# One decode step of an adaptive-layer-norm block: grouped output-weight loads and a rearranged last stage

## The chip, the cores and the metric

The kernel runs on one core of a Trainium2 chip, all data in float32. The metric is the device time of one execution in microseconds (us). Before the change the median of 3 runs is 394.72 us (393.41 to 396.38).

## The reference

One token for each of 4 batch rows goes through attention against a cache and a small token mixer, both modulated by a condition vector `c`:

```python
mod = (silu(c) @ w_mod).reshape(4, 6, 1, 512)      # sa, ca, ga, sb, cb, gb
h = layernorm(x) * (1 + ca) + sa
x = x + ga * A(h)        # q = h @ wq; 32 query heads, 8 KV heads, 4096 cached keys, Dh 128;
                         # softmax(q k^T / sqrt(128)) v, then @ wo (4096 x 512)
h = layernorm(x) * (1 + cb) + sb
x = x + gb * B(h)        # u = gelu(layernorm(h) * w1 + b1), F = 1792 values for each channel;
                         # y = sum over F of u * w2, + b2
```

The key and value caches are 4 x 8 x 4096 x 128 each, 67 MB apiece; with `wq`, `wo` and `w_mod` some 157 MB are read once.

## The kernel before

Batch row and KV head make a pair `i = 8 b + h`, 32 pairs in all. A pair needs one key tile and one value tile of 2 MB, each 128 partitions x 16 KB. They pass through a ring of five slots (`ring`), which also holds `wq` and the pieces `wm` of `w_mod`; a load into a slot is issued when the slot's last reader is done. All loads are issued by SyncE (SP) in the order in which they are written: the first two parts of `w_mod`, the small vectors (`sm`), `x`, four pieces of `wq`, three key tiles, and from there key tile, value tile, and for the first eight pairs the 1 MB of `wo` of head `i` (`load_v`). `wo` stays in memory for all four batch rows.

The schedule is written out by hand (`manual_schedule`): each engine runs its instructions in program order. In front of the main loop DVE clears a number of buffers (L67 to L89), while `sm` is loaded; then ACT and DVE form silu(c) (L115 to L120), PE multiplies with `w_mod` (L133), and the queries follow (L148).

The loop over pairs staggers scores (L213), softmax (L224 to L236), transposes of the probabilities (L243), values (L265) and the output projection (`project_a`, `project_b`). Behind each batch row of eight pairs the generator `epilogue` does layer norm and mixer of that row in small steps, one at each `next(epi)`. Its last two steps are the contraction of the remaining tiles of `u` with `w2` on PE, and `ZK` (L441) on DVE.

The last pairs stand behind the loop, each step by hand. `finish` then does row 3, with nothing left to overlap except the last steps of row 2's `epilogue`: `stats` and `gather` (a matmul that spreads the statistics to all partitions) twice, around `adaln`; `bcast` (L364), which spreads the row over the partitions; `affine`, in which ACT centres it (`hb`, L375) and DVE folds the reciprocal deviation into `w1` (`wr`); then 14 tiles of 512 values: scale and shift (DVE, or for the first two ACT), gelu (ACT, L461 and L466) and contraction with `w2` (PE, L387). Last come gate, residual and stores.

In `affine` the centring is `hb = pb + nm` with `nm = -mean` as an instruction of its own:

```python
        def center():
            dv.tensor_scalar(nm, mean, -1.0, None, op0=OP.mult)
            nc.scalar.activation(hb, pb, AF.Identity, bias=nm)
```

Of the kernel before, what the change touches and what calls it, by code (L numbers as in the profile page):

```python
# [8 lines left out]
F32 = mybir.dt.float32  # L9
I32 = mybir.dt.int32  # L10
AF = mybir.ActivationFunctionType
OP = mybir.AluOpType
# [3 lines left out]
B, D, HQ, HKV, SK, DH, F = 4, 512, 32, 8, 4096, 128, 1792  # L16
REP = HQ // HKV
NF = F // 128
EPS = 1e-5
P = 128  # L20
# [8 lines left out]


@with_exitstack
def adaln_decode(ctx: ExitStack, tc: tile.TileContext, small, x, wmod, wq, kT, v, wo, out):
    nc = tc.nc
    pad = ctx.enter_context(tc.tile_pool(name="pad", bufs=1))
    ring = ctx.enter_context(tc.tile_pool(name="ring", bufs=5))
    wos = ctx.enter_context(tc.tile_pool(name="wos", bufs=1))
    cst = ctx.enter_context(tc.tile_pool(name="cst", bufs=1))
    wk = ctx.enter_context(tc.tile_pool(name="wk", bufs=2))
# [4 lines left out]
    ps_e = ctx.enter_context(tc.tile_pool(name="ps_e", bufs=1, space=PSUM))  # L43
    ctx.enter_context(tc.manual_schedule())
    mm = nc.tensor.matmul
    dv = nc.vector

    neg1 = pad.tile([1, 96], F32, name="neg1")[:, 0:1]
    sm = cst.tile([P, NSM], F32, name="sm")
    xr = cst.tile([B, D], F32, name="xr")  # L50
    wm01 = ring.tile([P, 2, 4, D], F32, name="wm01", tag="kv")
    nc.sync.dma_start(wm01, wmod[0:2].rearrange("t p k n -> p t k n"))
    nc.sync.dma_start(sm, small)
    nc.sync.dma_start(xr, x)
    wqt = []
    for k in range(4):
        t = ring.tile([P, HQ * DH], F32, name=f"wq{k}", tag="kv")
        nc.sync.dma_start(t, wq[k * P:(k + 1) * P, :])
        wqt.append(t)
    w1, b1, w2 = sm[:, 0:NF], sm[:, NF:2 * NF], sm[:, 2 * NF:3 * NF]  # L60
# [2 lines left out]

    ident = cst.tile([P, P], F32, name="ident")
    make_identity(nc, ident)
    ones = cst.tile([P, P], F32, name="ones")
    dv.memset(ones, 1.0)  # L67
    dv.memset(neg1, -1.0)
# [15 lines left out]
    for i in range(3):  # L84
        t = cst.tile([P, 16, 32], F32, name=f"pT{i}")
# [1 line left out]
        pTs.append(t)  # L87
    pTl = cst.tile([P, 8, 4, 32], F32, name="pTl")
    dv.memset(pTl, 0.0)  # L89
    wo_t = [wos.tile([P, REP, D], F32, name=f"wo{h}") for h in range(HKV)]  # L90
    prep = cst.tile([P, 4, P], F32, name="prep")
    osb = cst.tile([P, B, P], F32, name="osb")
    sT8 = cst.tile([P, 4, B, 8], F32, name="sT8")

    def rsqrt(ve, n, tag, beside=None, out=None, times=None):
        y = wk.tile([n, 1], F32, name="y" + tag)
        t = wk.tile([n, 1], F32, name="t" + tag)
        q = wk.tile([n, 1], F32, name="q" + tag)
        dv.tensor_scalar(y.bitcast(I32), ve.bitcast(I32), -0.5, RS0, op0=OP.mult, op1=OP.add)
        if beside:  # L100
            beside()
        dv.scalar_tensor_tensor(t, y, ve, y, op0=OP.mult, op1=OP.mult)
        dv.scalar_tensor_tensor(y, t, RS1, y, op0=OP.subtract, op1=OP.mult)
        dv.scalar_tensor_tensor(t, y, ve, y, op0=OP.mult, op1=OP.mult)
        if times is not None:
            dv.tensor_scalar(out, times, y, None, op0=OP.mult)
        dv.scalar_tensor_tensor(q, t, RS2, t, op0=OP.subtract, op1=OP.mult)
        if times is not None:
            dv.scalar_tensor_tensor(out, q.to_broadcast(list(out.shape)), RS3, out, op0=OP.add, op1=OP.mult)
            return out  # L110
        dv.scalar_tensor_tensor(y, q, RS3, y, op0=OP.add, op1=OP.mult)
        return y
# [56 lines left out]
    def load_wm(t):  # L169
        n = 1 if t >= 4 else 2  # L170
        w = ring.tile([P, n, 4, D], F32, name=f"wm{t}", tag="kv")
        nc.sync.dma_start(w, wmod[t:t + n].rearrange("t p k n -> p t k n"))
        for e in range(n):
            WM[t + e] = w[:, e]

# [5 lines left out]
    def load_v(i):  # L181
        b, h = divmod(i, HKV)
        VT[i] = ring.tile([P, 32, DH], F32, name=f"v{i}", tag="kv")
        src = v[b, h].rearrange("(p j) d -> p j d", p=P)
        cuts = (0, 16, 24, 28, 32) if i == NS - 1 else (0, 16, 32) if i >= NS - 3 else (0, 32)
        for lo, hi in zip(cuts, cuts[1:]):
            nc.sync.dma_start(VT[i][:, lo:hi], src[:, lo:hi])
        if i < HKV:
            nc.sync.dma_start(wo_t[i], wo[i])
        if i == 2 or i == 4:  # L190
            load_wm(i)
        if i == NS - 1:
            load_wm(5)

    def modmm(pm, t):
        for k in range(4):
            for c in range(4):
                mm(pm[32 * c:32 * c + 32, :], sT8[:, k].rearrange("p b r -> p (b r)"),
                   WM[t][:, k, c * P:(c + 1) * P], start=(k == 0), stop=(k == 3))
# [132 lines left out]
    def stats(xin, b):  # L332
        st = wk.tile([P, 6], F32, name="st")
        dv.bn_stats(st, xin)
        sm_ = wk.tile([P, 4, 6], F32, name="stm")
        dv.tensor_mul(sm_, st.unsqueeze(1).to_broadcast([P, 4, 6]), ident.rearrange("p (c r) -> p c r", c=4)[:, :, 8 * b:8 * b + 1].to_broadcast([P, 4, 6]))
        return sm_

    def gather(sm_):
        pst = ps_m.tile([P, 24], F32, name="pst", tag="m")  # L340
        mm(pst, ones[0:1, :], epsr.rearrange("p a b -> p (a b)"), start=True, stop=False)
        mm(pst, ones, sm_.rearrange("p a b -> p (a b)"), start=False, stop=True)
        return pst

    def norm(pst):
        mv = wk.tile([P, 2], F32, name="mv")
        dv.bn_aggr(mv, pst)
        return mv[:, 0:1], mv[:, 1:2]

    def adaln(b, pst):  # L350
        mean, var = norm(pst)
        a = wk.tile([P, P], F32, name="a")
        h1 = wk.tile([P, P], F32, name="h1")
        r = rsqrt(var, P, "e", lambda: dv.scalar_tensor_tensor(
            a, XK[:, b], mean, prep[:, 3], op0=OP.subtract, op1=OP.mult))
        dv.scalar_tensor_tensor(h1, a, r, prep[:, 2], op0=OP.mult, op1=OP.add)
        return h1, stats(h1, b)

    def bcast(h1, b, pb=None):
        if pb is None:  # L360
            pb = ps_e.tile([P, 4, P], F32, name="phb", tag="e")
        for c in range(4):
            e = 32 * c + 8 * b
            mm(pb[:, c, :], ident[:, e:e + 1].to_broadcast([P, P]), h1, start=True, stop=True)  # L364
        return pb.rearrange("p c n -> p (c n)")

    def affine(pst, pb):
        mean, var = norm(pst)
        nm = wk.tile([P, 1], F32, name="nmean")
        hb = wk.tile([P, D], F32, name="hb")  # L370
        wr = wk.tile([P, NF], F32, name="wr")

        def center():
            dv.tensor_scalar(nm, mean, -1.0, None, op0=OP.mult)
            nc.scalar.activation(hb, pb, AF.Identity, bias=nm)  # L375

        rsqrt(var, P, "e", center, out=wr, times=w1)
        return hb, wr

    def expand(u, hb, wr, js):  # L380
# [63 lines left out]
    def finish(b, pg, xp, epi):  # L444
        uu = [ring.tile([P, 8, D], F32, name=f"uu{i}", tag="kv") for i in range(2)]
        U = [uu[j // 8][:, j % 8] for j in range(NF)]
        stm = stats(xp, b)
        dv.tensor_copy(XK[:, b], xp)
        pst = gather(stm)
        modmm(pg, 5)  # L450
        h1, stm = adaln(b, pst)
        pst = gather(stm)
        py = ps_s.tile([P, 8, P], F32, name="py3", tag="s")
        pb = bcast(h1, b, py[:, 4:])
        py = py[:, 0]
        next(epi)
        hb, wr = affine(pst, pb)
        for js in ((0,), (1,), (2, 3), (4, 5), (6, 7), (8, 9), (10, 11, 12), (13,)):
            j = js[0]
            if j < 2:  # L460
                nc.scalar.activation(U[j], hb, AF.Gelu_apprx_tanh, bias=b1[:, j:j + 1], scale=wr[:, j:j + 1])  # L461
                u = U[j].unsqueeze(1)
            else:
                u = uu[j // 8][:, j % 8:j % 8 + len(js)]
                expand(u, hb, wr, js)
                nc.scalar.activation(u, u, AF.Gelu_apprx_tanh)  # L466
            contract(py, u, js)
        next(epi)
        dv.tensor_mul(osb[:, :B - 1], ZK, pg.unsqueeze(1).to_broadcast([P, B - 1, P]))
        dv.tensor_add(osb[:, :B - 1], osb[:, :B - 1], XK[:, :B - 1])  # L470
        gbl = cst.tile([P, P], F32, name="gbl")
        dv.tensor_copy(gbl, pg)
        dst = out.rearrange("b (c n) -> b c n", c=4)
        for e in range(B - 1):
            nc.sync.dma_start(dst[e], osb[8 * e:P:32, e])
        dv.scalar_tensor_tensor(osb[:, b], py, b2, gbl, op0=OP.add, op1=OP.mult)
        dv.tensor_add(osb[:, b], osb[:, b], XK[:, b])
        nc.sync.dma_start(dst[b], osb[8 * b:P:32, b])

    def spread_gate():  # L480
        pgb = ps_m.tile([P, 4, P], F32, name="pgb", tag="m")
# [12 lines left out]
    for i in range(3):  # L494
        load_k(i)
    load_v(0)
    for i in range(2):
        scores(i)
# [3 lines left out]
    epi = iter(())  # L502
    for i in range(NS - 4):
# [14 lines left out]
        if i and i % HKV == 0:  # L518
            epi = epilogue(i // HKV - 1)
        for _ in range((1, 1, 1, 1, 2, 1, 1, 0)[i % HKV]):  # L520
            next(epi, None)
        if 3 <= i <= 5:
            t = i - 1
            pm = mod(t)
            dst = prep[:, {2: 1, 3: 2, 4: 3}[t]]
# [6 lines left out]
        if i == NS - HKV or i == NS - HKV + 1:  # L532
            e = 4 * (i - NS + HKV)
            fold_gate(gate, range(e, e + 4))
    n = NS - 4
# [71 lines left out]
```

## Time and profile before

| what | value |
| --- | --- |
| median of the runs | 394.72 us (393.41 to 396.38) |
| profiled execution: its time, its span | 393.18 us, 391.4 us |
| mean granted TensorE clock | 0.907 of full speed |
| PE busy | 305.5 us (78%), 3180 instructions |
| DVE busy | 180.7 us (46%), 494 instructions |
| ACT busy | 99.2 us (25%), 121 instructions |
| DMA | 157.80 MB in 12711 packets, 403 GB/s over the span |

A busy PE says little here: matmuls overlap, and their ends are modelled. More is read from the row of DMA rates over 40 slices of 9.8 us, from the chain of work that ended last, and from the order of the instructions behind the last transfer. An instruction that another engine's work covers costs nothing; one on that last chain costs its whole length.

### The profile page before, as it was taken

The numbers are of one execution on the slowest core, as the hardware profiler recorded it, in microseconds if no ns is written. First come the engines' busy times: TensorE is split into PE (matmuls) and PEld (weight loads), VectorE is DVE, ScalarE is ACT, GpSimd is POOL, SyncE is SP. The second block draws the span as 40 slices with busy tenths as digits, with TensorE's granted clock in tenths as the row PEclk, the third lists the DMA queues.
The fourth block names the chain that finished last, engine by engine and source line by source line (L and its number), as shares of the span: only waits on it lengthen the run. The fifth ranks groups of instructions, "written<-read, shape, count | busy, mean of one in ns | idle before, by whom it ended". The sixth has DMA issues, their size and how long they took to land.

```text
span 391.4 us, 7325 instructions
## 1 busy us (share of the span) xinstructions
PE 305.5 (78%) x3180; PEld 151.8 (39%) x3180; DVE 180.7 (46%) x494; ACT 99.2 (25%) x121; POOL 0.7 (0%) x6
## 2 busy tenths in 40 slices
PE   0975776949759498799798877998788678988883
PEld 0122333415425244344243332453334344555662
DVE  5222223304413234467464434675545367754466
ACT  1001211011101102025563210157531111573325
POOL 0000000000000000000000000000000000000000
PEclk9989688577968859899899998999999998999989
DMA  8999999999999999999999999999999999999800
GB/s 320 430 429 427 425 435 426 424 432 430 427 425 434 432 430 434 429 432 427 425 430 432 429 430 432 429 428 427 427 434 432 429 430 430 430 429 418 347 9 3
DMA packets 12711, 157.80 MB, mean 403 GB/s; under 512 B 1524, under 2 KB 1540, under 8 KB 1928
## 3 DMA queue, kind: packets, MB, share of 16 engines
q1 hardware_dynamic: 12680, 157.34, 94.6%
q8 instruction: 25, 0.41, 0.4%
q14 instruction: 6, 0.05, 0.0%
HBM read 157.32 MB, written 0.01 MB: 402 GB/s over the span
## 4 chain that ended last, share of the span: by engine, by line
DMA 69%; PE 23%; DVE 4%; ACT 2%; issue 1%; SPq 0%; ACTq 0%; DVEq 0%
DMA k<-in_kT 38%; DMA v<-in_v 29%; PE s L213 6%; PE pv L265 4%; PE s L133 3%; DMA sm<-in_small 2%; PE s L243 2%; ACT uu L466 1%; PE pt L290 1%; PE pa L301 1%; PE qs L148 1%; PE pb L231 1%; PE pq L308 1%; DVE mx L224 1%; PE py L387 1%
## 5 line engine op out<-in xcount | busy, mean ns | idle before, releaser
L213 PE MATMUL s<-k,QT 128*32 128x512 f32 x512 | 78.6, 742 | 48.2 <-DMA k<-in_kT 47.8
L236 ACT ACTIVATE p<-s,nm 128x1024 f32<-128x1024 f32 x32 | 35.7, 1115 | 214.2 <-DVE nm L233 214.1
L216 DVE TENSOR_REDUCE m<-s 128x1 f32<-128x1024 f32 x32 | 39.2, 1224 | 90.2 <-PE s L213 90.2
L265 PE MATMUL pv<-v,pT 128*32 128x256 f32 x960 | 63.9, 385 | 5.0 <-DMA v<-in_v 5.0
L213 PEld LDWEIGHTS s<-k,QT 128*32 128x32 f32 x512 | 15.5, 125 | 86.9 <-DMA k<-in_kT 56.9
L243 PE MATMUL s<-ident,p 128*128 128x128 f32 x256 | 38.3, 298 | 0.0
L243 PEld LDWEIGHTS s<-ident,p 128*128 128x128 f32 x256 | 33.3, 163 | 2.2 <-ACT p L236 1.2
L265 PEld LDWEIGHTS pv<-v,pT 128*32 128x32 f32 x960 | 26.6, 109 | 19.6 <-PE pm L222 5.5
L290 PEld LDWEIGHTS pt<-sel,po 128*128 128x128 f32 x126 | 18.2, 208 | 31.7 <-issue 24.2
L301 PE MATMUL pa<-wo,oT 128*32 128x512 f32 x192 | 29.0, 680 | 0.3 <-DVE oT L292 0.3
L269 DVE COPY po<-pv 128x256 f32<-128x256 f32 x30 | 12.7, 425 | 26.2 <-PE pv L265 26.2
L411 ACT ACTIVATE u<-u 128x1024 f32<-128x1024 f32 x21 | 21.2, 1052 | 4.6 <-DVE u L382 4.5
L224 DVE TENSOR_REDUCE mx<-pm 1x128 f32<-1x512 f32 x32 | 21.5, 672 | 0.7 <-PE pm L222 0.7
L290 PE MATMUL pt<-sel,po 128*128 128x4 f32 x126 | 21.0, 272 | 0.5 <-DVE po L269 0.5
L317 DVE TENSOR_TENSOR acc<-acc,pa 128x512 f32<-128x512 f32 x21 | 14.4, 687 | 13.6 <-PE pa L301 13.6
L382 DVE TENSOR_SCALAR u<-hb,wr,sm 128x512 f32<-128x512 f32 x42 | 20.2, 541 | 0.4
L236 ACT ACT_TABLE_LOAD x10 | 12.8, 1283 | 19.5 <-DVE nm L233 19.4
L133 PE MATMUL s<-wm,sT 128*4 128x512 f32 x16 | 9.8, 780 | 9.5 <-DVE sT L119 9.5
L231 PEld LDWEIGHTS pb<-neg,mx 1*128 1x128 f32 x64 | 9.4, 182 | 17.1 <-DVE mx L224 16.7
L231 PE MATMUL pb<-neg,mx 1*128 1x1 f32 x64 | 12.1, 256 | 4.1 <-DVE mx L224 4.1
L411 ACT ACT_TABLE_LOAD x11 | 14.1, 1283 | 4.3 <-DVE u L382 4.2
L249 DVE COPY pT<-s 128x128 f32<-128x128 f32 x31 | 9.0, 290 | 11.8 <-PE s L243 10.2
(136 smaller groups left out, 229.2 us busy)
## 6 DMA issues: line engine op xcount, KB each, us to landing
k<-in_kT SPq DMA_DIRECT2D x32, 2048.0 KB, 21.8
v<-in_v SPq DMA_DIRECT2D x29, 2048.0 KB, 23.3
wq<-in_wq SPq DMA_DIRECT2D x4, 2048.0 KB, 17.8
wo<-in_wo SPq DMA_DIRECT2D x8, 1024.0 KB, 24.0
v<-in_v SPq DMA_DIRECT2D x5, 1024.0 KB, 19.8
wm<-in_wmod SPq DMA_DIRECT2D x2, 2048.0 KB
wm<-in_wmod SPq DMA_DIRECT2D x2, 1024.0 KB, 14.6
v<-in_v SPq DMA_DIRECT2D x1, 512.0 KB, 20.9
```

The lines of the kernel that those rows point to most:

```text
L133: mm(s0[0:B, t * D:(t + 1) * D], sT[:, k, :], wm01[:, t, k, :], start=(k == 0), stop=(k == 3))
L213: mm(s[32 * c:32 * c + 32, n * 512:(n + 1) * 512], QT[:, b, h, :], KT[i][:, (n * 4 + c) * 512:(n * 4 + c + 1) * 512], start=True, stop=True)
L216: dv.tensor_reduce(m, s, axis=AX.X, op=OP.max)
L224: dv.tensor_reduce(mx, pm.rearrange("o (c r) -> o r c", c=4).unsqueeze(1).to_broadcast([1, 4, 32, 4]), axis=AX.X, op=OP.max)
L231: mm(pb, mx.rearrange("o c r -> o (c r)"), neg1, start=True, stop=True)
L236: nc.scalar.activation(p, s, AF.Exp, bias=nm, accum_out=l)
L243: nc.tensor.transpose(pt[:, k, :], p[:, k * P:(k + 1) * P], ident)
L265: mm(pv[32 * q:32 * q + 32, :], pTs[i % 3][:, k, :], VT[i][:, k * 2:(k + 1) * 2, :].rearrange("p j d -> p (j d)"), start=(k < 4), stop=(k ...
L290: mm(pt, po[:, c * DH:(c + 1) * DH], sel[:, c * REP:(c + 1) * REP], start=(c == 0), stop=(c == n - 1))
L301: mm(pa[32 * g:32 * g + 32, :], oT[:, g:g + 1].to_broadcast([P, 32]), wo_t[h][:, g, :], start=True, stop=True)
L382: dv.tensor_scalar(u[:, e, :], hb, wr[:, j:j + 1], b1[:, j:j + 1], op0=OP.mult, op1=OP.add)
L411: nc.scalar.activation(u, u, AF.Gelu_apprx_tanh)
```

## The change

Loads: `wo` is laid out by row of the head dimension, then by head. Heads 0 and 1, and heads 2 and 3, are loaded with 2 MB each; of heads 4 to 6 the rows 16 to 127 (heads 4 and 5 together, head 6), and head 7 with all rows. The first 16 rows of heads 4 to 6 come in four transfers of 4 rows x 24 KB, two with pair 1 and two with pair 3. Two parts of `w_mod` lie together for each row.

Last stage: ACT centres with scale -1 and the mean as bias, so that `hb` is negated, and `w1` is negated once at the start (`w1n`, DVE's first instruction). Row 2's contraction stands behind the first part of row 3's layer norm instead of behind the broadcast, and its `ZK` before the broadcast instead of behind the 14 tiles. Tiles 10, 11 and 12 are two groups instead of one. The last store is issued by ACT.

```diff
-    nc.sync.dma_start(wm01, wmod[0:2].rearrange("t p k n -> p t k n"))
+    nc.sync.dma_start(wm01, wmod[0])
...
     make_identity(nc, ident)
+    w1n = cst.tile([P, NF], F32, name="w1n")
+    dv.tensor_scalar(w1n, w1, -1.0, None, op0=OP.mult)
     ones = cst.tile([P, P], F32, name="ones")
...
-    wo_t = [wos.tile([P, REP, D], F32, name=f"wo{h}") for h in range(HKV)]
+    wo_all = wos.tile([P, HKV, REP, D], F32, name="wo")
+    wo_t = [wo_all[:, h] for h in range(HKV)]
...
-        nc.sync.dma_start(w, wmod[t:t + n].rearrange("t p k n -> p t k n"))
+        nc.sync.dma_start(w, wmod[t // 2, :, t % 2:t % 2 + n])
...
-        if i < HKV:
-            nc.sync.dma_start(wo_t[i], wo[i])
+        if i == 1 or i == 3:
+            for e in range(4 * i - 4, 4 * i + 4, 4):
+                nc.sync.dma_start(wo_all[e:e + 4, 4:7], wo_few[e:e + 4])
+        if i in wo:
+            src_ = wo[i]
+            n = src_.shape[1]
+            nc.sync.dma_start(wo_all[P - src_.shape[0]:, i:i + n], src_)
...
-        def center():
-            dv.tensor_scalar(nm, mean, -1.0, None, op0=OP.mult)
-            nc.scalar.activation(hb, pb, AF.Identity, bias=nm)
-
-        rsqrt(var, P, "e", center, out=wr, times=w1)
+        nc.scalar.activation(hb, pb, AF.Identity, bias=mean, scale=-1.0)
+        rsqrt(var, P, "e", out=wr, times=w1n)
...
         h1, stm = adaln(b, pst)
+        next(epi)
         pst = gather(stm)
+        next(epi)
         py = ps_s.tile([P, 8, P], F32, name="py3", tag="s")
         pb = bcast(h1, b, py[:, 4:])
         py = py[:, 0]
-        next(epi)
         hb, wr = affine(pst, pb)
-        for js in ((0,), (1,), (2, 3), (4, 5), (6, 7), (8, 9), (10, 11, 12), (13,)):
+        for js in ((0,), (1,), (2, 3), (4, 5), (6, 7), (8, 9), (10, 11), (12,), (13,)):
...
             contract(py, u, js)
-        next(epi)
...
-        nc.sync.dma_start(dst[b], osb[8 * b:P:32, b])
+        nc.scalar.dma_start(dst[b], osb[8 * b:P:32, b])
...
+    wo = a["A_wo"].reshape(HKV, REP, DH, D).transpose(2, 0, 1, 3)
...
+        "wo0": con(wo[:, 0:2]), "wo2": con(wo[:, 2:4]), "wo4": con(wo[16:, 4:6]),
+        "wo6": con(wo[16:, 6:7]), "wo7": con(wo[:, 7:8]), "wo_few": con(wo[:16, 4:7]),
```

More of the change, by code (lines that the diff above doesn't have):

```diff
@@ L31, in adaln_decode @@
 @with_exitstack
-def adaln_decode(ctx: ExitStack, tc: tile.TileContext, small, x, wmod, wq, kT, v, wo, out):
+def adaln_decode(ctx: ExitStack, tc: tile.TileContext, small, x, wmod, wq, kT, v, wo0, wo2, wo4, wo6, wo7, wo_few, out):
     nc = tc.nc
@@ L45, in adaln_decode @@
     mm = nc.tensor.matmul
+    wo = {0: wo0, 2: wo2, 4: wo4, 6: wo6, 7: wo7}
     dv = nc.vector
@@ L368, in affine @@
         mean, var = norm(pst)
-        nm = wk.tile([P, 1], F32, name="nmean")
         hb = wk.tile([P, D], F32, name="hb")
         wr = wk.tile([P, NF], F32, name="wr")
-        def center():
-            dv.tensor_scalar(nm, mean, -1.0, None, op0=OP.mult)
-            nc.scalar.activation(hb, pb, AF.Identity, bias=nm)
-        rsqrt(var, P, "e", center, out=wr, times=w1)
+        nc.scalar.activation(hb, pb, AF.Identity, bias=mean, scale=-1.0)
+        rsqrt(var, P, "e", out=wr, times=w1n)
         return hb, wr
@@ L592 @@
         "x": con(a["A_x"].reshape(B, D)),
-        "wmod": con(a["w_mod"].reshape(4, P, 6, D).transpose(2, 1, 0, 3)),
+        "wmod": con(a["w_mod"].reshape(4, P, 3, 2, D).transpose(2, 1, 3, 0, 4)),
         "wq": con(a["A_wq"]),
@@ L596 @@
         "v": con(a["A_v_cache"]),
-        "wo": con(a["A_wo"].reshape(HKV, REP, DH, D).transpose(0, 2, 1, 3)),
+        "wo0": con(wo[:, 0:2]), "wo2": con(wo[:, 2:4]), "wo4": con(wo[16:, 4:6]),
+        "wo6": con(wo[16:, 6:7]), "wo7": con(wo[:, 7:8]), "wo_few": con(wo[:16, 4:7]),
     }
```

## The prediction

> **What bounds the kernel now.** I read the page first: the 40 slices, the queues, the chain that ended last.
>
> ```profile
> GB/s 320 430 429 427 425 435 426 424 432 430 427 425 434 432 430 434 429 432 427 425 430 432 429 430 432 429 428 427 427 434 432 429 430 430 430 429 418 347 9 3
> DMA packets 12711, 157.80 MB, mean 403 GB/s; under 512 B 1524, under 2 KB 1540, under 8 KB 1928
> q1 hardware_dynamic: 12680, 157.34, 94.6%
> q8 instruction: 25, 0.41, 0.4%
> DMA 69%; PE 23%; DVE 4%; ACT 2%; issue 1%; SPq 0%; ACTq 0%; DVEq 0%
> ```
>
> From the second slice to the 36th the 16 DMA engines move about 430 GB/s without a dip: 157 MB set the time, and compute counts only in front of the stream and behind it. One engine moves 430/16 = 26.9 GB/s. The end of the stream in windows of one microsecond (columns: window, its length, busy time and instructions of PE, PEld, DVE, ACT, POOL, granted clock, DMA share, GB/s):
>
> ```profile
> 367.00:368.00 1.00, 0.60 (x8) 0.59 (x12) 0.34 (x1) 0.00 (x0) 0.00 (x0) 1.00 1.00 414
> 368.00:369.00 1.00, 1.00 (x41) 1.00 (x44) 0.16 (x1) 0.00 (x0) 0.00 (x0) 1.00 0.66 262
> 369.00:370.00 1.00, 1.00 (x47) 1.00 (x40) 0.00 (x0) 0.00 (x0) 0.00 (x0) 1.00 0.65 262
> 370.00:371.00 1.00, 1.00 (x30) 0.68 (x22) 0.10 (x1) 0.00 (x0) 0.00 (x0) 1.00 0.58 246
> 371.00:372.00 1.00, 0.75 (x8) 0.47 (x11) 0.35 (x2) 0.00 (x0) 0.00 (x0) 1.00 0.41 164
> 372.00:373.00 1.00, 1.00 (x33) 0.80 (x31) 0.00 (x0) 0.00 (x0) 0.00 (x0) 1.00 0.12 49
> ```
>
> The engines do not finish together. At 368 a third of them (0.34 x 16, five or six) has nothing left; the last ones work until about 372.4. A transfer over all 16 lands when the last engine has its rows, so each late landing waits for a late engine while early ones idle. Next the chain of waits in order of time (start, us, what):
>
> ```profile
> 324.10 21.65 DMA k<-in_kT
> ...
> 376.71 0.46 PE pst L342 x2
> 377.17 1.90 PE py L364 x8
> 379.09 0.70 ACT hb L375
> ...
> 386.56 1.12 PE py L387 x32
> ```
>
> The last transfer on the path is a key tile landing at 345.75 (324.10 + 21.65). Behind it lie 27 us of PE and then the serial last stage (DVE, PE, ACT) to the store. An earlier landing moves everything after it, as long as the last value pieces come earlier too, and they ride the same engines.
>
> **The change part by part.**
>
> *Who carries the rows.* How many engines does a transfer of 4 rows use? The window of the four output stores, 4 rows each, tells:
>
> ```profile
> DMA packets 32, 0.01 MB, mean 2 GB/s; under 512 B 16, under 2 KB 32, under 8 KB 32
> out<-osb SPq DMA_DIRECT2D x4, 2.0 KB
> ```
>
> 16 of the 32 packets are the 512-byte rows, the 16 others are under 512 B: four end marks for each transfer, so four engines for each, and for the new 4-row loads likewise. For heads 4 to 6 an engine carried 8 rows of 3 x 8 KB = 192 KB. Now each of 16 engines carries 7 rows (112/16), 168 KB, and four engines carry four rows of 24 KB more. Twelve engines lose 24 KB (24,576 bytes at 26.9 GB/s: 0.91 us) and four gain 72 KB (2.74 us). If the four are among those that finish at 368.0, they finish at 370.7, the late ones at 371.5 instead of 372.4: **-0.9 us**, and the same at the key tile's landing. If the four are late ones, it is +2.7 us; these are the bounds. The views name no engine. I take the early case: the late ones are marked by something that spares five or six engines, the 25 instruction fetches fit that, and the four engines of every small transfer are the same few.
>
> *Larger packets.* `wo` of two heads and `wmod` of two parts lie together now, 16 KB instead of 8 KB a packet: about 640 of 12,680 packets fewer. The rate in the stretches with 8 KB pieces bounds the gain:
>
> ```profile
> 355.00:360.00 5.00, 4.10 (x49) 2.88 (x49) 2.08 (x9) 2.49 (x3) 0.00 (x0) 1.00 1.01 421
> ```
>
> 421 against 430 GB/s is 2%; on the 10 MB that change their packets, 23 us of stream, that is at most 0.46 us, at least nothing: I take **-0.2 us**.
>
> *The head.* The new `w1n` is DVE's first instruction and waits for `sm`. All set-up that DVE did meanwhile queues behind it (timeline rows):
>
> ```profile
> 0.74 0.46 SPq L52 DMA_DIRECT2D wm<-in_wmod  x1
> 0.83 0.17 DVE L67 MEMSET ones<- 128x128 f32 x1 [0.83 <-PEq L599]
> ...
> 4.96 0.91 DVE L89 MEMSET pTl<- 128x1024 f32 x1 [0.16 <-issue]
> 8.55 0.22 ACT L115 ACTIVATE sg<-sm 128x16 f32<-128x16 f32 x1 [6.53 <-DMA sm<-in_small]
> 8.80 0.17 DVE L116 TENSOR_SCALAR sg<-sg 128x16 f32<-128x16 f32 x1 [2.93 <-ACT sg L115]
> ...
> 25.83 2.04 SPq L179 DMA_DIRECT2D k<-in_kT  x2
> ```
>
> The set-up runs from 0.83 to 5.87. Moved behind 8.55 and `w1n` it ends near 13.6, so DVE L116 starts some 4.85 us later, and the first matmuls, the queries and the key loads waiting for their ring slots with it. The tightest load is the second key tile, issued at 25.83, then at 30.7. Ahead of it lie 12.6 MB: 3.1 in the first slice of 9.8 us, the rest at 430 GB/s lasts until 31.9. The first load's bytes ran within about a microsecond of its issue at 0.74. So 0.2 us of slack is left: **0**, with a hole of up to 1 us as the other bound. Later loads are issued over 10 us ahead. The new semaphore waits of `wo` loads on SP's queue (with the next key load behind them) are for transfers eight issues older, and lie within that lead.
>
> *The last stage.* It starts after the landing, so its terms add. Timeline rows, two windows, and from the chain a group of the same eight 128x128 matmuls at the other clock:
>
> ```profile
> 358.40 1.04 PE s L243 x8
> 373.93 1.08 PE L198 MATMUL pgx<-wm,sT 128*32 128x128 f32 x32
> 375.00:376.00 1.00, 0.34 (x4) 0.23 (x2) 0.86 (x5) 0.00 (x0) 0.00 (x0) 1.00 0.00 0
> 376.71 0.46 PE L342 MATMUL pst<-stm,ones 128*128 128x24 f32 x2 [1.37 <-DVE stm L336]
> 377.00:378.00 1.00, 1.00 (x7) 1.00 (x7) 0.72 (x5) 0.00 (x0) 0.00 (x0) 0.50 0.06 16
> 377.58 0.14 DVE L374 TENSOR_SCALAR nmean<-mv 128x1 f32<-128x1 f32 x1
> 378.98 2.15 PE L387 MATMUL py<-u,sm 128*32 128x128 f32 x48
> 381.24 5.78 ACT L466 ACTIVATE uu<-uu 128x1024 f32<-128x1024 f32 x6
> 386.85 1.73 SPq L475 DMA_DIRECT2D out<-osb  x3
> 388.09 0.29 DVE L477 TENSOR_TENSOR osb<-osb,xk 128x128 f32<-128x128 f32 x1
> 388.68 0.50 SPq L478 DMA_DIRECT2D out<-osb  x1
> ```
>
> The 48 contraction matmuls of batch row 2 move from 378.98 to just behind L198's, at 375.0. At full clock they take 48 x 1.12/32 = 1.68 us, until 376.7: they fill PE's idle 1.37 us and push the statistics matmul (376.71) by 0.1 to 0.2, **+0.15 us**. They also keep PE busy where it idled before its clock fell to 0.50. The broadcast (L364) took 1.90 us at 0.50, its like took 1.04 at full clock: **-0.85 us**, at the least 0. The other bound: the contraction that follows loses those 48 matmuls as company, and a half clock there makes 16 matmuls, 0.56 us at 32 in 1.12, 1.1 us long where ACT delivers two tiles of 512 every 0.96 us (12 tiles in 5.78): 0.16 us for each of six pairs, up to +1 us.
>
> The Trainium skill (TensorE: Matmul & The Clock Gate, "What's actually happening") has a free-running window of about 3.4 us that sets the clock by the activity before; the trace agrees with the order (idle at 375, 0.50 at 377), and by that rule this term would differ from run to run.
>
> Centring: `nmean` was ready at 377.72, but ACT waited for the broadcast until 379.07: its removal gives **0**; it would give 0.14 were the broadcast done sooner. ZK's 0.35 us goes into DVE's wait for the statistics: 0. Splitting (10, 11, 12) lets PE start on 10 and 11 about half a microsecond (5.78/12) before ACT is done with 12, for one more ACT instruction: **-0.1 us**, bounds -0.25 and +0.2. The last store waited for SP, busy with three stores until 388.58, while its data stood at 388.38; from ACT it leaves then: **-0.3 us**, or +0.3 if ACT issues slower than SP's 0.50.
>
> Sum: -0.9 - 0.2 + 0 + 0.15 - 0.85 - 0.1 - 0.3 = **-2.2 us** on the profiled execution, 393.18 to 391.0. The median of the runs shown, 394.72, is 1.5 us above that execution; I forecast it at 392.5. Own range 390.0 to 395.2: the terms' bounds (-3.3 to +2) and the runs' scatter of 1.5.
>
> **The rivals.**
>
> *One way into SBUF (slower).* Rows e to e+3 go to neighbouring partitions, one for each of four engines. If these share one way into the memory with the rate of one engine, a 4-row load takes 3.65 us (98,304 bytes at 26.9 GB/s) instead of 0.91; all four 14.6 instead of 3.65, 10.95 us more on the four engines. They end at 370.7 + 10.95 = 381.7, 9.3 us behind today's last. With the other terms (-0.2, -1.1): +8.0, **402.7**. The stream loses from an extra 1.7 us on, the kernel over 1% from 6.9. For it: every load that ran at full rate had 128 rows, so nothing in the trace shows four engines at their own rates on neighbours. Against: no row shows a sharing either; the only 4-row load, `xr`, has 8 KB.
>
> The Trainium skill (SBUF — State Buffer, "Door 1: The DMA port swizzle") speaks for this rival: four adjacent partitions share one port, with 27.6 GB/s measured on partitions 0 to 3; by its figure a 4-row load takes an estimated 3.56 us. No run here shows it.
>
> *The four are late engines.* +2.7 - 0.2 - 1.1 = +1.4: **396.1**. For it: no view names the early ones. Against: the reason above.
>
> *The gain doesn't arrive.* A hole of 1 us behind the first key tile, or value pieces that still come as late, eats the stream's -1.1: the last stage alone, -1.1, **393.6**. Against: the value pieces ride the same engines as the key tile.
>
> **How the numbers follow.** Within 1% (3.9 us) is about what a measurement of this kernel can tell from no change. Forecast 0.56, of which 0.22 lies below 390.8 (the runs' scatter with the better bounds) and 0.34 within; shared way 0.28 (0.27 slower, 0.01 within, for a part of the price); late engines 0.08 and no arrival 0.08, both within. Faster 0.22, same 0.51, slower 0.27. The range reaches from 390.0 into the shared-way case up to 402.5, leaving out some 0.06 below and 0.13 above.
>
> **What would show it.** In the changed profile: a DMA share that stays near 1 until shortly before the end of the stream and then drops within about a microsecond (the balance), or falls to about 0.25 for many microseconds with 100 GB/s (the shared way), or to fewer engines 2.7 us longer (late ones). In the head: DVE's first step behind the set-up (L116 today) near 13.6, and still 430 GB/s in the third and fourth slice. A broadcast of some 1.04 us at clock 1.00, and a last store issued right behind DVE's last instruction. A stream that ends as late as before, or a fall below 420 GB/s in mid-run, would make the prediction wrong.

## The result and the profile after

The changed kernel takes 417.23 us (median of 4 runs, 415.53 to 419.2) against 394.76 (393.41 to 396.38): the ratio is 1.0575, with a 95% interval of 1.0534 to 1.0617. The profiled execution took 416.38 us with a span of 414.6, against 393.18 and 391.4. The 40 slices (10.4 us each now) and the totals of the queues, from the page of the changed kernel:

```profile
DMA  8999999999999999999999999999999999999700
GB/s 321 436 432 403 430 435 252 435 428 346 286 224 404 363 286 402 432 433 432 431 428 432 425 428 430 430 430 431 428 428 430 430 430 427 430 426 421 307 19 2
DMA packets 12023, 157.80 MB, mean 381 GB/s; under 512 B 1492, under 2 KB 1508, under 8 KB 1896
```

The bytes are the same, and there are fewer packets. But where the rate was even before, it now falls four times between 62 and 160 us. Taken against 430 GB/s, the slices from the second to the 35th lose 21.5 us (0.4 before), nearly all of the 22.5. Note the row above it: the DMA share stays at 9 all the while. The engines never run dry; their packets take longer. Windows of 4 us (length, busy PE, PEld, DVE, ACT, POOL, granted clock, DMA share, GB/s) say it in numbers:

```profile
64.00:68.00 4.00, 2.11 (x34) 1.21 (x34) 1.03 (x3) 0.44 (x1) 0.00 (x0) 1.00 1.00 158
112.00:116.00 4.00, 4.00 (x23) 1.51 (x16) 0.97 (x1) 0.00 (x0) 0.00 (x0) 0.55 1.02 236
120.00:124.00 4.00, 3.25 (x66) 2.12 (x66) 0.88 (x3) 1.20 (x2) 0.00 (x0) 1.00 0.94 205
148.00:152.00 4.00, 4.00 (x38) 1.99 (x30) 1.89 (x5) 0.00 (x0) 0.00 (x0) 1.00 1.08 350
```

SP's issues of the new loads (timeline: start, us, engine, line) tell which they are. A load's packets run some 18 to 30 us behind its issue:

```profile
41.35 0.67 SPq L194 DMA_DIRECT2D wo<-in_wo_few  x2
68.71 1.08 SPq L194 DMA_DIRECT2D wo<-in_wo_few  x2
84.18 0.33 SPq L198 DMA_DIRECT2D wo<-in_wo  x1
124.04 0.42 SPq L198 DMA_DIRECT2D wo<-in_wo  x1
```

The fall at 62 belongs to the first two 4-row loads, that at 97 to the second two. The ones at 105 to 128 and 140 to 160 belong to the loads of heads 4 and 5 and of head 6: these have 112 rows, and the prediction gave them no cost at all. From 160 us on all is as before. The chain shows what it does to the end:

```profile
348.64 21.72 DMA k<-in_kT
...
401.55 0.99 PE py L373 x8
402.56 0.70 ACT hb L381
```

The last key tile on the path lands at 370.36, 24.6 us later than before. From there to the end of the span there are 44.24 us, 1.41 less than before.

### The profile page after: what moved, and what is told of

It is laid out like the page before. It is cut to its first block, busy times and chain, and to the rows that moved or that the text cites. A ratio compares the mean times of both kernels' runs of the same rounds, so it can differ in the third digit from the quotient of the medians.

```text
span 414.6 us, 7323 instructions
## 1 busy us (share of the span) xinstructions
PE 299.7 (72%) x3180; PEld 148.0 (36%) x3180; DVE 180.1 (43%) x491; ACT 99.3 (24%) x122; POOL 0.7 (0%) x6
## 4 chain that ended last, share of the span: by engine, by line
DMA 66%; PE 24%; DVE 6%; ACT 2%; issue 1%; SPq 0%; ACTq 0%; DVEq 0%
DMA k<-in_kT 49%; DMA v<-in_v 16%; PE s L222 6%; PE pv L274 4%; PE s L137 2%; PE qs L152 2%; PE s L252 2%; DMA sm<-in_small 2%; PE pa L310 1%; PE pt L299 1%; ACT uu L472 1%; PE pq L317 1%; PE pb L240 1%; DVE acc L326 1%; DVE mx L233 1%
## 5 line engine op out<-in xcount | busy, mean ns | idle before, releaser
L222 PE MATMUL s<-k,QT 128*32 128x512 f32 x512 | 77.7, 735 | 66.8 <-DMA k<-in_kT 66.4
L252 PE MATMUL s<-ident,p 128*128 128x128 f32 x256 | 36.1, 287 | 0.0
L252 PEld LDWEIGHTS s<-ident,p 128*128 128x128 f32 x256 | 31.5, 156 | 2.7 <-issue 1.4
L310 PE MATMUL pa<-wo,oT 128*32 128x512 f32 x192 | 27.2, 640 | 0.3 <-DVE oT L301 0.2
L233 DVE TENSOR_REDUCE mx<-pm 1x128 f32<-1x512 f32 x32 | 21.5, 672 | 0.7 <-PE pm L231 0.7
L242 DVE COPY nm<-pb 128x1 f32<-128x1 f32 x32 | 5.1, 158 | 22.5 <-PE pb L240 22.5
```

The costliest lines, as they stand in the source:

```text
L222: mm(s[32 * c:32 * c + 32, n * 512:(n + 1) * 512], QT[:, b, h, :], KT[i][:, (n * 4 + c) * 512:(n * 4 + c + 1) * 512], start=True, stop=True)
L233: dv.tensor_reduce(mx, pm.rearrange("o (c r) -> o r c", c=4).unsqueeze(1).to_broadcast([1, 4, 32, 4]), axis=AX.X, op=OP.max)
L252: nc.tensor.transpose(pt[:, k, :], p[:, k * P:(k + 1) * P], ident)
L310: mm(pa[32 * g:32 * g + 32, :], oT[:, g:g + 1].to_broadcast([P, 32]), wo_t[h][:, g, :], start=True, stop=True)
```

## The experiments

**Taking the small loads apart.** Four kernels, with 393.64 us for the kernel before beside them. (Its medians beside the sets of runs below are 393.5 to 394.8, so a difference between runs of two sets is good to about 1 us.) The first gives heads 4 to 6 all their 128 rows again and keeps the rest of the change:

```diff
-        if i == 1 or i == 3:
-            for e in range(4 * i - 4, 4 * i + 4, 4):
-                nc.sync.dma_start(wo_all[e:e + 4, 4:7], wo_few[e:e + 4])
...
-        "wo0": con(wo[:, 0:2]), "wo2": con(wo[:, 2:4]), "wo4": con(wo[16:, 4:6]),
-        "wo6": con(wo[16:, 6:7]), "wo7": con(wo[:, 7:8]), "wo_few": con(wo[:16, 4:7]),
+        "wo0": con(wo[:, 0:2]), "wo2": con(wo[:, 2:4]), "wo4": con(wo[:, 4:6]),
+        "wo6": con(wo[:, 6:7]), "wo7": con(wo[:, 7:8]),
```

> The changed kernel with heads 4 to 6 loaded with all 128 rows (4 and 5 together, 6 alone) and without the four 4-row loads; all else as changed. Theory A (shared way): engines that write neighbouring rows share one way into SBUF at the rate of one engine, in the 4-row and in the 112-row loads; without both the whole loss goes: 393 to 395 us, before minus the 1.4 us of the last stage plus the 0.5 us hole in the head. Theory B (skew): the loss is the imbalance of the four engines and the waits it causes, no shared way: also 393 to 395. Theory C (layout): two heads together in HBM and in SBUF, or the waits of the two-head loads on SP, cost time by themselves: well above 400 us.

Measured 392.08 us, ratio 0.996 (0.9933 to 0.9987): a little below the 393 to 395 of theories A and B, and nothing is left for C. Its rates have no fall left in mid-run (page):

```profile
GB/s 310 434 434 434 427 432 428 429 430 434 419 439 430 429 430 429 430 429 429 428 428 430 429 429 432 429 431 430 429 432 429 430 430 429 431 425 419 380 31 3
```

So the split costs 417.2 - 392.1 = 25.1 us, and the rest of the change is a small gain. The second kernel keeps the split, but a 4-row load takes rows 4 apart instead of neighbours:

```diff
-            for e in range(4 * i - 4, 4 * i + 4, 4):
-                nc.sync.dma_start(wo_all[e:e + 4, 4:7], wo_few[e:e + 4])
+            for e in range(i - 1, i + 1):
+                nc.sync.dma_start(wo_all[e:16:4, 4:7], wo_few[e:16:4])
```

> The changed kernel, but each 4-row load takes rows 4 apart (e, e+4, e+8, e+12) in place of neighbours: same four engines, same bytes, same 24 KB packets, same 112-row loads. Theory A: a 4-row load falls from some 3 us and more per packet to about 0.9, the dip of the rate near 62 to 70 us (158 GB/s in its second half) is gone, and the total falls by 5 to 10 us, to 407 to 412. Theory B: same imbalance, so no change: 417 us.

Measured 407.8 us, ratio 1.0349 (1.0296 to 1.0402): which rows travel together decides over 9.4 us, though bytes, packets and transfers are the same. The third has no 4-row loads; the 112-row loads stay, and rows 0 to 15 of heads 4 to 6 are cleared instead of loaded (0.39 MB less, 0.9 us of stream):

```diff
+    nc.gpsimd.memset(wo_all[0:16, 4:7], 0.0)
...
-        if i == 1 or i == 3:
-            for e in range(4 * i - 4, 4 * i + 4, 4):
-                nc.sync.dma_start(wo_all[e:e + 4, 4:7], wo_few[e:e + 4])
```

> The changed kernel without the four 4-row loads: rows 0 to 15 of heads 4 to 6 are left out (cleared by GpSimd instead), 0.39 MB or 0.9 us of stream less; the 112-row loads stay. Theory A: the 112-row loads still put several engines on one way: stretches at about half rate near 105 to 124 and 140 to 156 us remain, 400 to 408 us. Theory B: 16 engines carry 7 rows each, no imbalance and no loss: 392 to 394 us.

Measured 402.02 us, ratio 1.0188 (1.0125 to 1.025). With the missing bytes that is 402.9, so the 112-row loads cost 10.8 us without any 4-row load. Page of the second, then of the third:

```profile
GB/s 318 433 434 410 431 429 430 429 431 431 214 319 431 291 346 431 436 425 431 429 429 425 431 433 428 428 433 429 428 433 428 431 429 428 429 427 422 370 13 2
```

```profile
GB/s 315 430 431 431 431 431 429 431 425 434 244 410 426 297 425 435 426 431 429 427 429 430 431 433 425 436 422 436 426 431 430 426 436 425 431 426 421 313 2 2
```

In the third the two falls (244, then 297) are those of the 112-row loads. With rows 4 apart nothing falls where the 4-row loads pass (62 and 97 us), but the 112-row falls are wider: 214 and 319, 291 and 346. From 100 to 112 us the third moves 252 GB/s at a DMA share of 1.00, 3.0 MB in all. That is more than the 1.8 MB of the load of heads 4 and 5, so other loads in flight are slowed with it.

The fourth is the first with `w1n` moved behind silu(c):

```diff
-    w1n = cst.tile([P, NF], F32, name="w1n")
-    dv.tensor_scalar(w1n, w1, -1.0, None, op0=OP.mult)
...
     dv.tensor_copy(sT8.rearrange(...), ...)
+    w1n = cst.tile([P, NF], F32, name="w1n")
+    dv.tensor_scalar(w1n, w1, -1.0, None, op0=OP.mult)
```

> As the kernel with all 128 rows and no 4-row loads, and w1n computed behind silu(c) instead of as DVE's first instruction. All theories: first matmuls near 9.7 us again, no dip of the rate at 32 to 34 us, 0.5 us less than with the early w1n: 392.5 to 394.5 us, about 1.4 us below the kernel before.

Measured 392.04 us, ratio 0.9967 (0.9937 to 0.9998): the place of `w1n`, for which 0.5 us was expected, can't be told in the total.

**The loads by themselves.** A kernel of loads alone, one at a time, each answered by a DVE copy of one element (`sink`); nothing of the block is computed (abridged):

```python
t = pool.tile([P, 6144], F32, name=name, tag="few")
nc.sync.dma_start(t[0:hi, 0:4096], v[n, 0:hi])          # hi = 128, 112, 96, ...
...
for i, r in enumerate(rows):                            # 0:4 and 4:8, or 0:16:4 and 1:16:4
    nc.sync.dma_start(t[r], few[4 * (n + i):4 * (n + i) + 4])
nc.sync.dma_start(u, v[n])                              # a load of 2 MB behind them
```

> Loads alone, one after the other, each issued when the one before has landed; nothing of the block is computed. Rows of 16 KB from partition 0: 128, 112, 96, 64, 32 and 16 of them; then 4 rows of 24 KB on neighbouring partitions, 4 apart, 32 apart; then a 2 MB load alone, behind two 4-row loads of neighbours, and behind two with rows 4 apart. Each twice. Theory A: with 2 us of fixed time, 128 rows land in about 7 us, 112 rows in 9 to 11 rather than 6.3, 4 neighbours in 5.6, 4 rows 4 apart in 2.9; the 2 MB load is 3 to 7 us later behind neighbours and about 2 behind rows apart. Theory B (only skew): time to landing goes by rows for each engine: 112 rows 6.3, 96 rows 5.6, 64 rows 4.4, and 4 rows 2.9 in all three patterns.

Its timeline, from one execution with each load twice; the bracket has DVE's wait for the load, which is issued as the wait begins:

```profile
16.82 0.14 DVE L23 COPY sink<-full 1x1 f32<-1x1 f32 x1 [7.83 <-DMA full<-in_v]
...
26.28 0.14 DVE L23 COPY sink<-oneless 1x1 f32<-1x1 f32 x1 [9.32 <-DMA oneless<-in_v]
...
45.06 0.14 DVE L23 COPY sink<-twoless 1x1 f32<-1x1 f32 x1 [8.84 <-DMA twoless<-in_v]
...
61.87 0.14 DVE L23 COPY sink<-half 1x1 f32<-1x1 f32 x1 [7.26 <-DMA half<-in_v]
...
92.41 0.14 DVE L23 COPY sink<-near 1x1 f32<-1x1 f32 x1 [5.51 <-DMA near<-in_few]
97.54 0.14 DVE L23 COPY sink<-near 1x1 f32<-1x1 f32 x1 [4.99 <-DMA near<-in_few]
...
101.10 0.14 DVE L23 COPY sink<-apart 1x1 f32<-1x1 f32 x1 [3.42 <-DMA apart<-in_few]
...
109.14 0.14 DVE L23 COPY sink<-far 1x1 f32<-1x1 f32 x1 [4.30 <-DMA far<-in_few]
...
139.48 0.14 DVE L23 COPY sink<-bnear 1x1 f32<-1x1 f32 x1 [13.03 <-DMA bnear<-in_v]
...
162.32 0.14 DVE L23 COPY sink<-bapart 1x1 f32<-1x1 f32 x1 [9.33 <-DMA bapart<-in_v]
```

A load of 112 rows (`oneless`) takes longer than one of 128 with a seventh more bytes: 9.3 (the second 9.7) against 7.8 us. It is not the only such shape: 96 rows (`twoless`) take 8.8 and 9.3 us, and 64 rows (`half`) 7.3, nearly as long as 128. Theory B, which goes by the rows of each engine, wanted 6.3, 5.6 and 4.4. Four neighbours of 24 KB take 5.0 to 5.5 us, four rows 4 apart 3.4 to 3.5, four rows 32 apart (`far`) 4.3 to 4.5. So neighbours cost 1.5 to 2.1 us more than rows 4 apart; four engines sharing the rate of one would cost 2.7 more (3.65 - 0.91).

The Trainium skill (SBUF — State Buffer, "Door 1: The DMA port swizzle") gives four adjacent partitions one port, partitions 4 apart different ports, and a row 32 further on the same one (64 further on another); the order 3.4, 4.3, 5.0 agrees with one, two and four rows on a port.

The last two rows are the point the prediction lacked. A load of 2 MB behind two loads of neighbours lands 13.0 us after the first issue, behind two of rows 4 apart after 9.3, both times. Windows of that stretch (columns: window, its length, DVE, POOL, granted clock, DMA share, GB/s):

```profile
130.00:131.00 1.00, 0.00 (x0) 0.00 (x0) 1.00 0.87 131
131.00:132.00 1.00, 0.00 (x0) 0.00 (x0) 1.00 1.17 131
132.00:133.00 1.00, 0.00 (x0) 0.00 (x0) 1.00 0.84 115
133.00:134.00 1.00, 0.00 (x0) 0.00 (x0) 1.00 0.33 82
134.00:135.00 1.00, 0.00 (x0) 0.00 (x0) 1.00 0.97 410
```

Twelve engines that have only the 2 MB load would make 12 x 26.9 = 323 GB/s. All 16 together make 82 to 131. From 128 to 134 us the mean is 137 GB/s at a DMA share of 0.93, so nearly all engines have a packet under way and still get little through; then the rate jumps to 410. Behind rows 4 apart there is no such stretch. So the four engines that load the neighbours hold up the others too; by what means, no run shows.

**One cost at a time in the whole kernel.** Two kernels, with 393.74 us for the kernel before beside them. In both every load has its 128 rows, and the 16 rows are loaded once more in the change's places, 4 apart or as neighbours; the full loads write the same data over them later. Against the kernel with full rows (`e:e + 4` instead of `e:16:4`, and the change's range, for neighbours):

```diff
+        if i == 1 or i == 3:
+            for e in range(i - 1, i + 1):
+                nc.sync.dma_start(wo_all[e:16:4, 4:7], wo_few[e:16:4])
         if i in wo:
```

> All loads of 128 rows as in the run with full rows, and beside them the same 16 rows of heads 4 to 6 once more in four transfers of 4 rows that lie 4 apart, at the places of the changed kernel (the later full loads write the same data over them; 0.39 MB more, 0.9 us of stream). It gives the four engines of these transfers 96 KB more each, 3.65 us. Theory A, the 4-row loads cost by themselves what the differences of the earlier runs give (407.8 - 402.9 = 4.9 us): 392.1 + 0.9 + 4.9 = 397.9, range 396.5 to 399. Rival B, the four engines are among the early ones, as the prediction took it, and rows on different ways hinder nobody: 392.1 to 393.3. Rival C, the four are late ones and only that costs: 392.1 + 3.65 = 395.7.

> The same with the rows of each 4-row load neighbours, as the change has them, and still every other load with 128 rows. Theory A, the two costs of the change add up (neighbours 417.2 - 402.9 = 14.3 us): 392.1 + 0.9 + 14.3 = 407.3, range 405 to 409, with dips of the rate only near 62 to 70 and 97 to 104 us. Rival B, neighbours cost as much as they do only in company with the 112-row loads: the time of rows 4 apart, within 2 us.

Rows apart: 395.23 us, ratio 1.0028 (1.0003 to 1.0053), so 3.15 us over full rows: neither the additive theory (397.9) nor the free one, but nearly the price of late engines (395.7). Neighbours: 402.46 us, ratio 1.0208 (1.0178 to 1.0237), 9.5 us without the bytes, where theory A wanted 14.3 and rival B no more than rows apart cost: neighbours cost much without any 112-row load, too, but less than beside them. Ends of the stream with full rows, then with rows apart besides (windows, columns as in the first fence of windows):

```profile
370.00:371.00 1.00, 1.00 (x26) 0.56 (x14) 0.26 (x1) 0.00 (x0) 0.00 (x0) 1.00 0.60 246
372.00:373.00 1.00, 1.00 (x34) 0.80 (x22) 0.13 (x1) 0.00 (x0) 0.00 (x0) 1.00 0.02 8
```

```profile
370.00:371.00 1.00, 0.69 (x12) 0.68 (x16) 0.30 (x2) 0.00 (x0) 0.00 (x0) 1.00 0.73 307
372.00:373.00 1.00, 1.00 (x48) 1.00 (x40) 0.00 (x0) 0.00 (x0) 0.00 (x0) 1.00 0.18 72
...
374.00:375.00 1.00, 0.75 (x15) 0.58 (x18) 0.19 (x2) 0.00 (x0) 0.00 (x0) 1.00 0.06 25
```

Two more engines are busy at 370 (0.73 against 0.60 of 16), so some of the four were early ones; but about one engine (0.06 of 16) works on beyond 374, where full rows ended at 372 and the 0.9 us of added bytes would end near 373. These ends are not on the chain that ended last in either run. The time goes by when the tiles land. Scores of the same two key tiles, with full rows, then with rows apart besides (timelines):

```profile
114.33 3.64 PE L219 MATMUL s<-k,QT 128*32 128x512 f32 x16 [6.72 <-DMA k<-in_kT]
286.11 1.92 PE L219 MATMUL s<-k,QT 128*32 128x512 f32 x16 [1.52 <-DMA k<-in_kT]
```

```profile
117.31 3.23 PE L222 MATMUL s<-k,QT 128*32 128x512 f32 x16 [8.80 <-DMA k<-in_kT]
289.25 1.92 PE L222 MATMUL s<-k,QT 128*32 128x512 f32 x16 [1.51 <-DMA k<-in_kT]
```

From the second pair of 4-row loads until 309 us the tiles land some 3 us later (2.4 to 3.4 where both kernels' scores wait), with no fall in the rates. One late engine among the four fits that, if a landing waits for the last engine; no view names an engine. The match with 3.65 is not clean: at 318 us the key tile is only 1.8 us late, from there on no transfer is on the chain of this execution, and PE adds to the delay with 16 score matmuls in 3.39 us at a granted clock of 0.50 (1.92 with full rows).

**The order of the two.** The single costs, 10.8 and 9.5, leave 4.8 us of the 25.1. Two kernels put the 4-row loads behind the 112-row loads, in pairs 10 and 12 (393.5 us for the kernel before). The first against the changed kernel (the second has `range(i - 10, i - 8)` and `e:16:4`):

```diff
+    nc.gpsimd.memset(wo_all[0:16, 4:7], 0.0)
...
-        if i == 1 or i == 3:
-            for e in range(4 * i - 4, 4 * i + 4, 4):
+        if i == 10 or i == 12:
+            for e in range(4 * i - 40, 4 * i - 32, 4):
                 nc.sync.dma_start(wo_all[e:e + 4, 4:7], wo_few[e:e + 4])
```

> The changed kernel with its 4-row loads of neighbours moved behind the 112-row loads, to pairs 10 and 12 (rows 0 to 15 of heads 4 to 6 are zero until then, so batch row 0 is computed without them; the bytes are the changed kernel's). The costs measured singly are 10.8 us for the 112-row loads and 9.5 us for the 4-row loads (402.46 - 392.1 - 0.9), together 20.3; the changed kernel lost 25.1. Theory A, the missing 4.8 us come from the 112-row loads meeting engines that the 4-row loads have put out of step: 392.1 + 20.3 = 412.4, range 411 to 414, and the dips of the 112-row loads as shallow as without 4-row loads. Rival B, the two costs add to more in any order: 416 to 418.

> The same with rows 4 apart (batch row 0 again without rows 0 to 15 of heads 4 to 6). Theory A: 392.1 + 10.8 + 2.2 (395.23 - 392.1 - 0.9) = 405.1, range 404 to 406. Rival B, order doesn't matter: 407 to 408.5, as with the loads ahead of the 112-row loads.

Neighbours behind: 409.52 us, ratio 1.04 (1.0365 to 1.0435), 7.7 less than the changed kernel. Rows apart behind: 402.3 us, ratio 1.0222 (1.0187 to 1.0258), 5.5 less than ahead, and no more than without any 4-row loads (402.9 with the bytes). Both lie some 3 us below what theory A gave, so in this order the single costs don't add up in full, and far from B. Pages of the two:

```profile
GB/s 314 436 433 425 430 438 424 428 431 409 228 436 422 301 423 434 430 323 395 434 359 430 428 433 428 431 426 432 431 430 423 434 433 428 426 427 419 275 6 2
```

```profile
GB/s 315 434 431 431 429 431 430 425 433 429 239 428 425 288 422 434 428 429 429 428 433 427 431 431 428 429 428 430 426 438 423 434 429 431 426 427 420 342 10 2
```

The 112-row falls are back to one slice each (228 and 301, 239 and 288), as without 4-row loads. The neighbours have falls of their own further back (323 and 395, 359), the rows apart none. So it is shown that a 112-row load costs more once 4-row loads have gone ahead of it. That they do it by leaving four engines behind the others is the reading that fits; no run isolates it.

**The small gains.** Three more kernels. The kernel before has only the edits of `affine` and `finish` (with `w1n` late), or only those of the `wmod` and `wo` loads, all with 128 rows; and the kernel with full rows and late `w1n` has its last store on SP:

```diff
-        nc.scalar.dma_start(dst[b], osb[8 * b:P:32, b])
+        nc.sync.dma_start(dst[b], osb[8 * b:P:32, b])
```

> The kernel before with the rearranged last stage alone (contraction, centring with w1n behind silu(c), split of the last group, last store from ACT); every load as before. Theory A, the whole 1.55 us gained by the run with full rows is the last stage: 391.8 to 392.4. Rival B, the larger packets gave part of it, 0.2 us or more as the prediction took it: 392.3 to 393.2. A difference from the run with full rows under 0.3 us tells neither.

> The kernel before with the larger packets alone (output weights of two heads, modulation weights of two parts together), every load of 128 rows, last stage as before. Theory A, what the runs of today suggest: the larger packets give 1.0 us (392.5 against 393.7 with the last stage alone): 392.4 to 393.0. Rival B, the prediction's -0.2 us: 393.3 to 393.9.

> The run with full rows and late w1n, but the last store from SP as before. The prediction gave the ACT store -0.3 us; the profile of the changed kernel shows an ACT issue of 1.10 us against 0.50 on SP, landing 1.65 us behind the end of DVE's last instruction. Theory A, ACT's slower issue eats the gain: within 0.3 us of 392.0, and in the profile a last landing between 1.5 and 2.0 us behind DVE's last instruction. Rival B, SP's three earlier stores still delay it: 392.3 or more, landing over 2.0 us behind DVE's last instruction.

Last stage alone: 393.7 us, ratio 0.9985 (0.9961 to 1.0009). Larger packets alone: 393.51 us, ratio 0.9992 (0.9962 to 1.0021). The first lies above both of its forecasts, the second where the prediction's -0.2 wanted it, but neither can be told from no change, and these two runs don't tell how the 0.4% that they bring together divides. Full rows with the store on SP: 392.53 us, ratio 0.9958 (0.9934 to 0.9983), the same as from ACT within the scatter; both profiled executions span 390.0 us. The timelines of the last stores, full rows with the store on ACT, then on SP:

```profile
387.15 0.29 DVE L479 TENSOR_TENSOR osb<-osb,xk 128x128 f32<-128x128 f32 x1
387.47 1.11 ACTq L480 DMA_DIRECT2D out<-osb  x1
```

```profile
385.73 1.73 SPq L477 DMA_DIRECT2D out<-osb  x3
...
387.26 0.29 DVE L479 TENSOR_TENSOR osb<-osb,xk 128x128 f32<-128x128 f32 x1
387.58 0.50 SPq L480 DMA_DIRECT2D out<-osb  x1
```

SP is free at 387.46 now, ahead of DVE's end at 387.55, because its three other stores start 1.82 us ahead of that end; before, it was 1.53 (388.38 - 386.85), and SP came free 0.2 behind it. The store leaves 0.03 us behind DVE on either queue; ACT's issue takes 1.11 us, SP's 0.50.

Full rows, with `w1n` early or late and the store on either queue, beat both the kernel before, by 0.3 to 0.4% with intervals that end just below 1, and the changed one.

## Why the prediction was wrong

*Who carries the rows* is the step that failed: -0.9, with +2.7 as its worst. It counted bytes for each engine and took each engine's rate as its own, whatever rows it writes. The runs showed +25.1 in its place: 10.8 for the two 112-row loads, 9.5 for the neighbours, and 4.8 as the remainder, which goes with their meeting. The prediction's own sign of being wrong, a fall below 420 GB/s in mid-run, came four times. Three things were missing.

First, the 112-row loads had no line of the sum. Seven rows an engine instead of eight were costed as a gain, although the text says that every load that ran at full rate had 128 rows. By itself such a load takes 9.3 us against 7.8. That 1.5 us, even with the saved bytes, is far from 10.8 for two loads; in the stream the loads beside them are slowed as well, and why by so much stays open.

The Trainium skill (DMA: Bandwidth & Descriptors, "The descriptor swizzle") says of a 128-partition transfer that each engine writes a port of its own; seven neighbouring rows straddle the groups of four, so engines would meet in one port. The falls from 430 to 244 and 297 GB/s would fit; no run here shows which engine writes which row.

Second, *One way into SBUF* was the right rival, at 0.28, for neighbours. A shared way fits the loads by themselves, 5.0 to 5.5 against 3.4 us, if at a lower price than it gave. But it priced 10.95 us on four engines, with twelve running free, and took only the end of the four as the loss. What came is another shape: it held up the others too, so the DMA share stayed near 1 at 158 GB/s, where the prediction looked for a share of 0.25 with 100 GB/s. Its 402.7 lies at the run with neighbours alone (402.46) by luck. There about half of the cost is this hold-up (slices 271, 391 and 406 in its rates, 5.2 us); the rest, it seems, is the lag of the four engines, which no view names:

```profile
GB/s 319 428 433 430 433 431 271 430 430 391 406 430 428 433 424 435 428 431 431 425 433 426 428 436 426 430 433 426 431 430 428 431 431 431 425 421 423 267 7 2
```

Third, the four as early engines: half right. In the run with rows apart besides some seem to be early, but about one is not, and the tiles land some 3 us later. The price of *The four are late engines* (3.65 us for 96 KB) is near the 3.15 of that run, with the reservations made there.

*Larger packets*, -0.2: the packets alone measured -0.3 us, with an interval from -1.5 to +0.8; not contradicted. *The head* was right to a few tenths. In the changed kernel's timeline and windows:

```profile
8.62 0.17 DVE L68 TENSOR_SCALAR w1n<-sm 128x14 f32<-128x14 f32 x1 [8.62 <-DMA sm<-in_small]
13.44 0.11 DVE L120 TENSOR_SCALAR sg<-sg 128x16 f32<-128x16 f32 x1
24.10 6.89 SPq L183 DMA_DIRECT2D k<-in_kT  x2
...
32.00:34.00 2.00, 2.00 (x24) 0.60 (x20) 0.00 (x0) 0.00 (x0) 0.00 (x0) 1.00 1.00 344
```

DVE's first step behind the set-up stands at 13.44 (13.6 was foretold); the second key tile's issue ends at 24.10 + 6.89 = 30.99, so it starts near the 30.7 foretold. The slack of 0.2 us was a hole of about 0.4, (430 - 344)/430 of 2 us, within the bound of 1. It doesn't always come: with full rows and the same head the key loads began 1.1 us earlier, and this window has 426 GB/s. The run with late `w1n` shows no difference in the total.

*The last stage*, -1.1 in all, measured -1.41 from the last key landing to the end of the span, in one profiled execution; the run with the last stage alone gained 0.6 us, with an interval from -1.5 to +0.4. The broadcast took 0.99 us where -0.85 made it 1.04; it takes 0.99 with the last stage alone, too, and 1.70 with the packets alone. The last store's -0.3 was put down to the wrong edit: the wait for SP goes with the new order of the stage, not with the store's move to ACT, and in the profile of the unmoved store nothing is left of it. *The gain doesn't arrive* has no run for it: with full rows the kernel gains 0.4%.

One sum of the prediction is off. Its terms' bounds add up to -2.7 and +1.8 with the first term at -0.9, and to +5.4 with that at +2.7, not to -3.3 and +2. Even +5.4 is far from the measured +22.5.

## What to carry to other kernels

A transfer that doesn't cover all 128 partitions must not be costed by bytes over engines: first ask which rows are written at the same time, and take a price from a load of that shape, measured in the stream in which it will run: by itself a 112-row load was only 1.5 us longer. The DMA share didn't show the loss here (1.00 at 158 GB/s), since the page counts the time that packets take, waits included; the GB/s row did. And where 16 engines end 4 us apart, work that is put on a few of them may well be on the path: 96 KB more on four engines cost some 3 us.

## What the runs showed of the hardware

- Two loads of four neighbours hold up the other engines too: 137 GB/s at a DMA share of 0.93 over 6 us, and 3.7 us (13.03 - 9.33) for the 2 MB load behind them.
- Loads of 112 and 96 rows of 16 KB land later (9.3 to 9.7 and 8.8 to 9.3 us) than one of 128 rows (7.8).
- The cost of a 112-row load depends on what went before it: its falls took two or three slices behind 4-row loads and one without; 5.5 us lie between rows 4 apart ahead of and behind the 112-row loads.
- The issue of a 4-row store takes 1.11 us on ACT's queue and 0.50 on SP's.
